# Fewer TensorE instructions in the opening of a delta-attention and two-mixture kernel, and the second solve on VectorE

## The chip, the cores and the metric

One core of a Trainium2 chip runs the kernel. The metric is the device time of one execution in microseconds, as the median of three runs. In the text PE is TensorE (PEld its weight loads), DVE VectorE, ACT ScalarE, POOL GpSimd and SP the SyncE queue that starts most transfers.

## The reference

Batch 4, 8 heads, 768 positions, head width 48. For each head a 48 x 48 state is walked through in time:

```
y[t]   = q[t] @ state
state += beta[t] * outer(k_n[t], v[t] - k_n[t] @ state)     # k_n is k over its norm
x  = y as 3072 x 384
x  = (silu(x @ w_gate) * (x @ w_val)) @ w_out               # 384 -> 1536 -> 384
out = mish(x @ w_in) @ w2_out                               # 384 -> 2048 -> 384
```

The weights come as float64 and are made float32 on the chip.

## The kernel before, in words

The sequence is cut into chunks of 32 positions; 4 batches of 32 make 128 partitions. Three chunks are a step (t = 0 to 7). Inside a chunk the recurrence is a triangular system: from the grams of k with k (`gram_pair`) a solve on VectorE gives a 32 x 32 inverse for each head and chunk. The grams of k with q become the matrix p, masked on GpSimd (`att_mask`). Then, chunk after chunk: `read` (k and q times the state, labels r and y), the v that remains, `att_solved` (z, the inverse times v), `att_out` (p times z added to y, label o), `att_update` (k times z added to the state, label u), and `x_out` (the output transposed and split into a high and a low part, xh and xl, label x).

The first mixture runs one step behind: step t's twelve gate and value groups (g0, v0, g1, ...: nine matmuls each, three products of high and low parts) and downs (x0, x1, ...) stand on TensorE while step t+1's attention is put between them. Each group's result leaves one PSUM bank: g by ScalarE (s), v by VectorE (h). The weights of the first mixture are 36 pieces, each made from float64 in passes: two on ScalarE (`conv_begin`, tile raw), one on VectorE (`conv_step`, tile f, L572), a high part on ScalarE (w1h, L591) and a low part on GpSimd (w1l, L592).

The order is written by hand. `START` is a list of words for the opening, taken one after the other: each word issues its instructions, on whichever engines, in this order, and each engine's queue keeps it. `kg0` is the k grams of chunk 0, `Kg0` those of step 1, `qg0` k with q; `sq`, `norm`, `turn`, `scale`, `diag` prepare the solve; `s2` is two steps of step 0's solve on VectorE, `P5` five steps of step 1's on GpSimd, `S` the same on VectorE; the solve is done in halves (`solve_half`, 15 steps, L276 and L283) and the quarter that joins the halves is made by TensorE (`ja`, `jb`; `Ja`, `Jb` for step 1); `back` transposes the result (L287 to L289); `vs` multiplies v by the norm on GpSimd, `qm` masks p there; `cb`, `d`, `t` are conversion passes; `h12` is twelve warm-up matmuls. `z0>` begins a word (its matmuls), `>z0` goes on with it (its evacuation). `EARLY1` names words due at a time counted in groups of the first mixture's step 0 (0.7 is near the end of g0). `plan` gives due times to the other steps. DMA starts stand on SP's queue, the first ten weight fetches on ScalarE's (`FETCH`).

The prediction's terms go through `START`, `EARLY1`, `att_mask` (L195), `square_sums` (L206), `att_solved` (L365), `att_out` (L384), `att_update` (L402), `gram_pair` (L449) and the loads after L791.

Of the kernel before, what the change touches and what calls it, by code (L numbers as in the profile page):

```python
# [7 lines left out]
F32 = mybir.dt.float32  # L8
# [5 lines left out]
ALU = mybir.AluOpType  # L14
# [10 lines left out]
FIRST = 0  # L25
FB = 3
START = """
sq0 sq1 sq2 h12 kg0 kg1 norm kg2 turn0 scale diag s1 Kg0 s2 Kg1 s2 Kg2 s2 qg0 s2 qg1 s2 qg2 s5 vs0 vs1 vs2 fetch go cb2 qm0 qm1 qm2 back0 clear
ja0> ja1> >ja0 jb0> ja2> >ja1 turn1 nb d1 >jb0 z0> >ja2 jb1> ns1 y0 >z0 u0> o0> ns2 t1 >u0 >jb1 r1> jb2> y1 ne >r1 z1> gam1 >o0 >jb2 x0> d1 >z1 u1> o1> scale diag >x0 >x0 t1 P5
>u1 r2> y2 >r2 z2> >o1 x1> d1 >z2 u2> o2> >x1 >x1 P5 t1 >u2 >o2 x2> qg3 >x2 >x2 P5 d1 t1 qm3 d1 t1 done  # L30
"""
FILL = (0.1, 0.8)
W2AT = (4.5, 2.0, 6)
W2F = 2.0
W2G = 1.7
RAWS = 2
FETCH = 10
RAWB = 4
MOST = 2
GRAMS = ("g", "x20", "x21", "x22") * 5  # L40
JOINS = ("x21", "x22") * 3
XTS = ("v", "x22", "v")
AHEAD = 1
EARLY1 = "0.7:back1 1.3:Ja0> 1.3:Ja1> 1.6:>Ja0 1.6:>Ja1 2.3:Ja2> 2.3:Jb0> 2.6:>Ja2 2.6:>Jb0 3.3:Jb1> 3.3:Jb2> 3.6:>Jb1 3.6:>Jb2 4.0:qg4 4.6:qm4 6.3:qg5 7.3:qm5"
GRAM2 = 6.0


# [12 lines left out]
def tile_delta_attention_moe_moe(  # L60
# [54 lines left out]
    w1h, w1l = [list(x) + [None] * 3 for x in zip(*map(w1_tiles, range(J1 - 3)))]  # L115
# [20 lines left out]
    ss, rs, n_sys = [t_tmp[:, C * i:C * i + C] for i in range(3)]  # L136
    state = at.tile([128, B, NP, 2, D], F32, name="state")

    z_s = at.tile([128, H, 2, D], F32, name="z_s")
    y_s = [at.tile([128, DM], F32, name=f"y{i}") for i in range(NCH)]  # L140

    w2d = [dram.tile([128, 6, 128], F32, name=f"w2d{j}") for j in range(J2)]
# [37 lines left out]
    def k_of(n):  # L180
        return lent_k if n == 2 else k_s[n % 2]
# [11 lines left out]
    spare = {"gram": list(GRAMS), "join": list(JOINS), "xt": list(XTS)}  # L193

    def att_mask(t, c):  # L195
        p = p_nat[num(t, c) % 5]
        nc.gpsimd.tensor_tensor(
            out=p, in0=p, in1=mask.unsqueeze(1).to_broadcast([128, H, C]), op=ALU.mult
        )

    def turn_g(t):
        nc.vector.transpose(
# [1 line left out]
        )  # L204

    def square_sums(c):  # L206
        sq = m1.tile([128, H, D], F32, tag="h", name="sq")
        kk = k_of(c)
        nc.vector.tensor_tensor(out=sq, in0=kk, in1=kk, op=ALU.mult)
        nc.vector.tensor_reduce(out=n_nat[:, c * H:c * H + H], in_=sq, op=ALU.add, axis=mybir.AxisListType.X)  # L210

    def norms(diag):
# [151 lines left out]
    @phased  # L364
    def att_solved(t, c):  # L365
        z = psa.tile([128, H, D], F32, tag="a", name="z")
        for h in range(H):
            for b in range(B):
                bs = slice(C * b, C * b + C)
                nc.tensor.matmul(  # L370
                    out=z[bs, h], lhsT=t_of(t)[bs, :, c * H + h], rhs=v_s[c][bs, h, :], start=True, stop=True
                )
        yield
        for x in range(2):
            if starting and x:
                nc.vector.tensor_scalar(
                    out=z_s[:, :, x, :], in0=z, scalar1=turn_of[:, x:x + 1], scalar2=None, op0=ALU.mult
                )
            else:
                nc.scalar.activation(out=z_s[:, :, x, :], in_=z, func=AF.Identity, scale=turn_of[:, x:x + 1])  # L380
        load(1, num(t + 1, c))

    @phased
    def att_out(t, c, hold):  # L384
        y = hold["y"]
        for h in range(H):
            for b in range(B):
# [61 lines left out]
    def gram_pair(t, c, which=(0, 1), raw=False):  # L449
        n = num(t, c)  # L450
        ws = slice(which[0], which[-1] + 1)
        pss = [bank([128, NP, 2, C], "gram") for _ in range(2)]
        for p in range(NP):
            for b in range(B):
                bs = slice(C * b, C * b + C)
                for par in range(2):
                    rows = slice(64 * par, 64 * par + D)
                    nc.tensor.matmul(  # L458
                        out=pss[par][bs, p, ws],
                        lhsT=kq_of(n)[rows, p, 0, bs],  # L460
                        rhs=kq_of(n)[rows, p, ws, bs],
                        start=True,
                        stop=True,
                    )
# [338 lines left out]
    for b in range(B):
        ub = upper[C * b:C * b + C, :]
# [40 lines left out]
    def solve_next(t, n, eng):  # L845
# [231 lines left out]
```

## Time and profile before

| | us |
|---|---|
| median of three runs (1077.42 to 1078.47) | 1077.65 |
| the profiled execution | 1075.51 |
| its span, first to last instruction | 1073.4 |
| TensorE busy (96% of the span) | 1031.5 |
| VectorE busy (48%) | 512.9 |
| ScalarE busy (37%) | 398.3 |
| GpSimd busy (18%) | 190.2 |

Matmul times are modelled and overlap, so a busy TensorE is not at its peak. A row of the timeline gives start, length, engine, line, operation, what is written and read, count, and in brackets the idle time of the engine before it with what ended it; "issue" means that the profile shows no wait. The granted clock is a share of 2.4 GHz; 0.50 is the lower level, 1.2 GHz.

### The profile page before, as it was taken

To read this page: it belongs to the slowest core of one execution; us is meant where nothing else is said; L and a number is where in the kernel's file an instruction comes from. 1 tells how busy PE (TensorE), PEld (TensorE's weight loads), DVE (VectorE), ACT (ScalarE), POOL (GpSimd) and SP (SyncE) were. 2 spreads that over 40 slices of the span, in tenths; PEclk is the share of its full clock that TensorE was granted. 3 is DMA by queue.
4 is the path that set the end of the run, shared out by engine and by line. 5 is a ranking of instruction groups with operands and counts; after the bars stand their busy time and mean duration, and the time that the engine had idled before them with its cause. 6 is when DMAs were issued, how large, how long until landed. Compare 5 with 4: busy or idle time off the path is not lost.

```text
span 1073.4 us, 29430 instructions
## 1 busy us (share of the span) xinstructions
PE 1031.5 (96%) x12980; PEld 988.7 (92%) x12980; DVE 512.9 (48%) x1113; ACT 398.3 (37%) x871; POOL 190.2 (18%) x222
## 2 busy tenths in 40 slices
PE   4779799999999999999999999999999999999998
PEld 4668699889989999999999999999999999999998
DVE  8555896785884885866852243212121222212111
ACT  2259744224224234243222345333333333323232
POOL 3276632211211312212211121000000000000000
PEclk6779899999999999999999999999999999999999
DMA  7246624215206125132010044001000000100000
GB/s 213 93 152 211 202 85 154 72 45 167 72 32 188 45 72 154 44 109 68 16 60 2 16 148 140 23 7 39 24 23 23 23 31 16 38 7 30 1 23 23
DMA packets 43183, 77.52 MB, mean 72 GB/s; under 512 B 4272, under 2 KB 30000, under 8 KB 43056
## 3 DMA queue, kind: packets, MB, share of 16 engines
q1 hardware_dynamic: 41904, 72.50, 21.6%
q10 hardware_dynamic: 1152, 3.15, 0.9%
q8 instruction: 102, 1.67, 0.7%
q14 instruction: 25, 0.20, 0.1%
HBM read 59.90 MB, written 15.73 MB: 70 GB/s over the span
## 4 chain that ended last, share of the span: by engine, by line
PE 81%; DVE 6%; issue 1%; ACT 1%; ACTq 0%; DVEq 0%
PE o L635 19%; PE h L635 19%; PE v L635 12%; PE x L707 12%; PE g L635 11%; PE z L370 1%; PE ks L350 1%; PE ds L412 1%; PE y L389 1%; PE y L350 1%; DVE t_tmp L324 1%; PE gram L458 1%; DVE t_sys L331 1%; DVE h L686 1%; DVE state L429 1%
## 5 line engine op out<-in xcount | busy, mean ns | idle before, releaser
L983 DVE TENSOR_TENSOR gl<-gg,gh 128x384 fp32r<-128x384 f32 x128 | 71.4, 558 | 319.2 <-ACT gh L982 319.2
L692 POOL TENSOR_TENSOR hp<-h,hp 128x384 fp32r<-128x384 f32 x96 | 99.8, 1039 | 419.4 <-ACT hp L691 419.4
L977 ACT ACTIVATE gg<-h 128x384 f32<-128x384 f32 x128 | 62.9, 492 | 264.8 <-PE h L635 264.8
L707 PE MATMUL x<-hp,w1h 128*128 128x384 f32 x576 | 132.1, 338 | 1.4 <-ACT hp L691 1.4
L635 PE MATMUL o<-w2l,gh 128*128 128x384 f32 x384 | 129.3, 337 | 0.0
L635 PE MATMUL o<-w2h,gh 128*128 128x384 f32 x384 | 129.2, 336 | 0.0
L635 PE MATMUL o<-w2h,gl 128*128 128x384 f32 x384 | 129.2, 336 | 0.0
L691 ACT CAST hp<-h 128x384 fp32r<-128x384 f32 x96 | 49.3, 513 | 168.5 <-DVE h L686 168.4
L707 PEld LDWEIGHTS x<-hp,w1h 128*128 128x128 f32 x576 | 101.1, 188 | 3.9 <-ACT hp L691 2.1
L635 PE MATMUL h<-x2h,w2h 128*128 128x384 f32 x384 | 88.0, 337 | 0.0
L635 PE MATMUL h<-x2l,w2h 128*128 128x384 f32 x384 | 87.8, 336 | 0.0
L635 PE MATMUL h<-x2h,w2l 128*128 128x384 f32 x384 | 87.7, 336 | 0.0
L686 DVE TENSOR_TENSOR h<-s,v 128x384 f32<-128x384 f32 x96 | 52.8, 549 | 72.7 <-PE v L635 72.1
L678 ACT ACTIVATE s<-g 128x384 f32<-128x384 f32 x96 | 46.9, 489 | 101.6 <-PE g L635 101.6
L324 DVE TENSOR_TENSOR t_tmp<-t_sys,g_sys 128x31 f32<-128x31 f32 (+15 forms) x186 | 80.9, 435 | 4.5
L331 DVE TENSOR_TENSOR t_sys<-t_sys,t_tmp 128x31 f32<-128x31 f32 (+15 forms) x186 | 74.8, 402 | 6.4
L635 PE MATMUL g<-xh,w1h 128*128 128x384 f32 x288 | 69.2, 349 | 7.5 <-ACT s L678 6.5
L635 PEld LDWEIGHTS o<-w2h,gh 128*128 128x128 f32 x384 | 72.1, 188 | 0.0
L635 PEld LDWEIGHTS o<-w2h,gl 128*128 128x128 f32 x384 | 72.1, 188 | 0.0
L635 PEld LDWEIGHTS o<-w2l,gh 128*128 128x128 f32 x384 | 72.1, 188 | 0.0
L635 PE MATMUL v<-xh,w1h 128*128 128x384 f32 x288 | 67.8, 343 | 2.9 <-DVE h L686 2.6
L635 PEld LDWEIGHTS h<-x2h,w2h 128*128 128x128 f32 x384 | 68.9, 188 | 0.0
(129 smaller groups left out, 1762.9 us busy)
## 6 DMA issues: line engine op xcount, KB each, us to landing
raw<-in_w_second_dram SPq DMA_DIRECT2D x32, 384.0 KB, 4.0
raw<-in_w_first_dram SPq DMA_DIRECT2D x28, 384.0 KB, 3.9
kqT<-in_kq_dram SPq DMA_DIRECT2D x18, 512.0 KB, 3.6
w2d<-f SPq DMA_DIRECT2D x32, 192.0 KB, 4.1
w2raw<-w2d SPq DMA_DIRECT2D x16, 384.0 KB, 2.9
v<-in_v_dram SPq DMA_DIRECT2D x24, 192.0 KB, 2.9
x2d<-xs SPq DMA_DIRECT2D x24, 192.0 KB, 1.9
x2raw<-x2d SPq DMA_DIRECT2D x24, 192.0 KB, 2.4
```

Source lines behind the costliest of these rows:

```text
L324: nc.vector.tensor_tensor(out=tmp, in0=t_sys[:, 0:m, j:j + 1].to_broadcast([128, m, n]), in1=g_sys[:, j:j + 1, j + 1:C].to_broadcast([128, ...
L331: nc.vector.tensor_tensor(out=sl, in0=sl, in1=tmp, op=ALU.subtract)
L350: nc.tensor.matmul(out=ps[bs, 2 * p:2 * p + 2], lhsT=kqt[:, p, w, bs], rhs=state[:, b, p], start=not w or p == 0, stop=not w, skip_group_c ...
L370: nc.tensor.matmul(out=z[bs, h], lhsT=t_of(t)[bs, :, c * H + h], rhs=v_s[c][bs, h, :], start=True, stop=True)
L635: nc.tensor.matmul(out=ps, lhsT=a, rhs=b, start=start and i == 0, stop=stop and i == len(seq) - 1)
L678: nc.scalar.activation(out=s, in_=ps, func=AF.Silu)
L686: nc.vector.tensor_tensor(out=h, in0=g_t.pop(j), in1=ps, op=ALU.mult)
L691: nc.scalar.copy(out=hh, in_=h)
L692: nc.gpsimd.tensor_tensor(out=hl, in0=h, in1=hh, op=ALU.subtract)
L707: nc.tensor.matmul(out=x2[kk], lhsT=w[j][:, 6 + kk, :], rhs=m, start=j == 0 and i == 0, stop=j == J1 - 1 and i == 2,)
L977: nc.scalar.activation(out=gg, in_=ps, func=AF.Mish)
L983: nc.vector.tensor_tensor(out=gl, in0=gg, in1=gh, op=ALU.subtract)
```

## The change: what it does

- k and q are loaded together, and the grams of k with k and k with q come out of one pass with 64 columns (`kq`), for chunks 0 to 4; chunk 5 has k in the opening (`kg5`) and q in the mixture. p of the first three chunks goes into lent weight space, unmasked.
- The first three outputs (`att_out` at t = 0) use one 128 x 128 matrix for a head, which GpSimd builds as p times a block-diagonal mask of 1024 elements a partition, and 8 matmuls of 48 columns for 32 of 32 x 32 blocks; z is kept once more whole (`z_all`) for it.
- z_s is laid out by parity first, and both its halves come from ScalarE.
- The v products and masks of the opening stand behind the first solve on GpSimd. The squares of k are made by ScalarE.
- Step 1's solve is on VectorE: seven steps in the opening, eight in g0 of the mixture; its transposes come at 0.9 and its joins at 2.9 to 4.6 groups. The last state update of step 0 is added at 1.6 groups.
- jb2 stands behind z1, more warm-up matmuls stand between the grams, the weight fetches are all on SP's queue, three conversion pieces may be under way (`MOST`), and six rather than five pieces are done in the opening.

```diff
-sq0 sq1 sq2 h12 kg0 kg1 norm kg2 turn0 scale diag s1 Kg0 s2 Kg1 s2 Kg2 s2 qg0 s2 qg1 s2 qg2 s5 vs0 vs1 vs2 fetch go cb2 qm0 qm1 qm2 back0 clear
-ja0> ja1> >ja0 jb0> ja2> >ja1 turn1 nb d1 >jb0 z0> >ja2 jb1> ns1 y0 >z0 u0> o0> ns2 t1 >u0 >jb1 r1> jb2> y1 ne >r1 z1> gam1 >o0 >jb2 x0> d1 >z1 u1> o1> scale diag >x0 >x0 t1 P5
->u1 r2> y2 >r2 z2> >o1 x1> d1 >z2 u2> o2> >x1 >x1 P5 t1 >u2 >o2 x2> qg3 >x2 >x2 P5 d1 t1 qm3 d1 t1 done
+sq0 sq1 sq2 h12 kq0 kq1 norm kq2 h8 turn0 scale diag s3 kq3 h6 s3 kq4 h6 s3 kg5 h12 s6 go cb3 back0 clear vs0 qm0 vs1 qm1 vs2 qm2 qm3 qm4
+ja0> ja1> >ja0 jb0> ja2> >ja1 turn1 nb d1 >jb0 z0> >ja2 jb1> ns1 y0 >z0 u0> o0> t1 ns1 d1 >u0 >jb1 r1> y1 ns1 ne >r1 z1> >o0 jb2> gam1 scale diag S1 >z1 t1 d1 u1> o1> S2 >u1 >jb2 r2> x0> y2 t1 >x0 >r2 >x0 d1 >o1 z2> x1> >z2 t1 S2 o2> u2> >x1 >x1 >o2 x2> h4 d1 >x2 >x2 S2 t1 d1 t1 done
-FETCH = 10
+FETCH = 0
-MOST = 2
+MOST = 3
-XTS = ("v", "x22", "v")
+XTS = ("x22",) * 3
-EARLY1 = "0.7:back1 1.3:Ja0> 1.3:Ja1> 1.6:>Ja0 1.6:>Ja1 2.3:Ja2> 2.3:Jb0> 2.6:>Ja2 2.6:>Jb0 3.3:Jb1> 3.3:Jb2> 3.6:>Jb1 3.6:>Jb2 4.0:qg4 4.6:qm4 6.3:qg5 7.3:qm5"
+EARLY1 = "0.3:S4 0.6:S4 0.9:back1 1.6:>u2 2.9:Ja0> 2.9:Ja1> 3.2:>Ja0 3.2:>Ja1 3.6:Ja2> 3.6:Jb0> 3.9:>Ja2 3.9:>Jb0 4.3:Jb1> 4.3:Jb2> 4.6:>Jb1 4.6:>Jb2 6.0:qg5 6.3:qm5"
...
-    z_s = at.tile([128, H, 2, D], F32, name="z_s")
+    z_s = at.tile([128, 2, H, D], F32, name="z_s")
...
+        n = num(t, c)
+        p = p_of(n)
+        if n < NCH:
+            nc.gpsimd.tensor_tensor(
+                out=lent_p[n][:, 0:H].rearrange("q h (b t) -> q h b t", b=B),
+                in0=p.unsqueeze(2).to_broadcast([128, H, B, C]),
+                in1=same.unsqueeze(1).to_broadcast([128, H, B, C]),
+                op=ALU.mult,
+            )
...
-        nc.vector.tensor_tensor(out=sq, in0=kk, in1=kk, op=ALU.mult)
+        nc.scalar.activation(out=sq, in_=k_of(c), func=AF.Square)
...
+        if starting and c == NCH - 1:
+            nc.scalar.copy(out=z_all, in_=z)
         for x in range(2):
-            if starting and x:
-                nc.vector.tensor_scalar(
-                    out=z_s[:, :, x, :], in0=z, scalar1=turn_of[:, x:x + 1], scalar2=None, op0=ALU.mult
-                )
-            else:
-                nc.scalar.activation(out=z_s[:, :, x, :], in_=z, func=AF.Identity, scale=turn_of[:, x:x + 1])
+            nc.scalar.activation(out=z_s[:, x], in_=z, func=AF.Identity, scale=turn_of[:, x:x + 1])
+        if starting and c < NCH - 1:
+            nc.vector.tensor_copy(out=z_all, in_=z)
...
+            if t == 0:
+                nc.tensor.matmul(
+                    out=y[:, h], lhsT=lent_p[c][:, h, :], rhs=z_all[:, h, :], start=c == 0 and h == 0,
+                    stop=h % 2 == 1, skip_group_check=True,
+                )
+                continue
...
-            pss = [psm.tile([128, NP, 2, D], F32, tag=x, name="ds") for x in ("g", "x20")]
+            tags = ("x20", "x21") if c == NCH - 1 else ("g", "x20")
+            pss = [psm.tile([128, NP, 2, D], F32, tag=x, name="ds") for x in tags]
...
-        load_kq(c, slice(0, 1))
+        load_kq(c)
     nc.sync.dma_start(out=beta_s, in_=beta)
+    for c in range(NCH):
+        load(1, c)
+    for n in range(NCH, 2 * NCH):
+        load_kq(n)
+    for n in range(RAWB):
+        fetch(n)
...
-    for n in range(NCH, 2 * NCH):
-        load_kq(n, slice(0, 1))
-    for c in range(NCH):
-        load_kq(c, slice(1, 2))
-        load(1, c)
-    fetch(0, nc.sync)
-    fetch(1, nc.sync)
-    for n in range(NCH, 2 * NCH):
-        load_kq(n, slice(1, 2))
...
-        "kg": lambda n: gram_pair(0, n, (0,)),
-        "Kg": lambda n: gram_pair(1, n, (0,)),
+        "kq": lambda n: gram_pair(n // NCH, n % NCH, (0, 1), True),
+        "kg": lambda n: gram_pair(n // NCH, n % NCH, (0,)),
```

## Rows read from the trace of the kernel before

**Rows 1.** The chain that ended last: shares of the span, and in order of time (start, us):

```profile
PE 81%; DVE 6%; issue 1%; ACT 1%; ACTq 0%; DVEq 0%
...
148.07 1.56 PE v L635 x9
```

**Rows 2.** Busy time by stretch, granted clock, DMA share, GB/s; last two VectorE alone:

```profile
26.43:40.11 13.68, 9.32 (x459) 8.38 (x452) 6.64 (x19) 4.89 (x11) 1.97 (x2) 0.50 0.25 89
40.11:60.83 20.72, 13.46 (x589) 10.96 (x585) 11.21 (x27) 6.97 (x16) 11.89 (x28) 0.91 0.39 131
60.83:74.71 13.88, 12.55 (x283) 11.55 (x284) 8.25 (x13) 9.06 (x20) 9.47 (x14) 0.57 0.57 170
74.71:81.58 6.87, 6.64 (x211) 5.86 (x211) 2.09 (x5) 3.46 (x9) 4.04 (x5) 1.00 0.29 79
...
130.50:1073.40 942.90, 935.06 (x9968) 902.90 (x9968) 429.60 (x922) 327.17 (x705) 119.45 (x115) 1.00 0.19 59
...
8.00:10.00 2.00, 1.37 (x83) 1.06 (x83) 1.69 (x10) 1.20 (x4) 0.00 (x0) 0.50 1.12 309
...
16.76:23.80 7.04, 6.36 (x20) 0.50 0.42 107
...
65.25:67.88 2.63, 2.63 (x5) 0.50 0.66 214
```

**Rows 3.** Timeline of TensorE, from the opening to the stop before g8:

```profile
13.24 1.78 PE L458 MATMUL gram<-kqT 48*32 48x32 f32 x127 [3.39 <-issue]
18.84 0.74 PE L458 MATMUL gram<-kqT 48*32 48x32 f32 x47 [3.82 <-issue]
...
26.12 1.89 PE L298 MATMUL join<-lent_tn,g_nat 32*32 32x16 f32 x113 [0.68 <-issue]
...
30.02 0.91 PE L298 MATMUL join<-lent,tT_nat 32*32 32x16 f32 x49 [1.79 <-issue]
...
44.85 0.54 PE L370 MATMUL z<-v,lent_tn 32*32 32x48 f32 x19 [0.59 <-issue]
...
57.07 0.55 PE L440 MATMUL xt<-ident,y 128*128 128x128 f32 x3 [0.60 <-ACT y L398]
...
59.41 0.46 PE L458 MATMUL gram<-kqT 48*32 48x32 f32 x29 [1.38 <-issue]
...
60.83 1.33 PE L635 MATMUL g<-xh,w1h 128*128 128x384 f32 x3 [0.96 <-ACT xh L445]
...
130.50 1.33 PE L635 MATMUL g<-xh,w1h 128*128 128x384 f32 x3 [5.38 <-ACT s L678]
```

**Rows 4.** DMA queues of the page: packets, MB, share of 16 engines:

```profile
q8 instruction: 102, 1.67, 0.7%
```

**Rows 5.** Timeline of VectorE:

```profile
13.99 0.24 DVE L276 TENSOR_TENSOR t_tmp<-t_sys,g_sys 128x78 f32<-128x78 f32 x1
14.27 0.75 DVE L283 TENSOR_TENSOR t_sys<-t_sys,t_tmp 128x78 f32<-128x78 f32 x1
...
55.71 2.07 DVE L429 TENSOR_TENSOR state<-state,ds 48x384 f32<-48x384 f32 x4 [0.52 <-PE ds L412]
...
114.04 0.94 DVE L219 TENSOR_SCALAR t_tmp<-t_tmp 128x32 uint32<-128x32 uint32 x1
115.02 0.18 DVE L222 TENSOR_SCALAR t_tmp<-t_tmp 128x32 uint32<-128x32 uint32 x1
```

**Rows 6.** Timeline of GpSimd:

```profile
14.02 0.90 POOL L314 TENSOR_TENSOR v<-v,n_nat 128x384 f32<-128x384 f32 x1 [7.28 <-DVE t_sys L283]
...
20.79 0.72 POOL L197 TENSOR_TENSOR p<-p,mask 128x256 f32<-128x256 f32 x1 [3.22 <-ACT p L471]
...
26.49 0.96 POOL L870 MEMSET t_sys<- 128x1024 f32 x1 [1.00 <-DVE lent_tn L289]
...
113.92 1.02 POOL L592 TENSOR_TENSOR w1l<-f,w1h 128x384 fp32r<-128x384 f32 x1
```

**Rows 7.** Timeline of ScalarE:

```profile
60.28 0.50 ACT L445 CAST xh<-xt 128x384 fp32r<-128x384 f32 x1
```

More of the change, by code (lines that the diff above doesn't have):

```diff
@@ L113, in w1_tiles @@
         return [pool.tile([128, 9, 128], F32R, tag=f"{x}{j}", name=f"w1{x}{j}") for x in "hl"]
-    w1h, w1l = [list(x) + [None] * 3 for x in zip(*map(w1_tiles, range(J1 - 3)))]
+    w1h, w1l = [list(x) + [None] * 5 for x in zip(*map(w1_tiles, range(J1 - 5)))]
     k_s = [at.tile([128, H, D], F32, name=f"k{i}") for i in range(2)]
@@ L172, in tile_delta_attention_moe_moe, with p_of @@
     lent_tn = lent_tn[:, 0:C * 32].rearrange("p (a b) -> p a b", a=C)
+    lent_p = [w1.tile([128, 9, 128], F32, tag=x, name=f"lent_p{x}") for x in ("l9", "h8", "l8")]
+    same = lent_p[0][:, 8, :].rearrange("p (b t) -> p b t", b=B)
+    lent_w = w1.tile([128, 9, 128], F32, tag="h7", name="lent_w")
+    z_all = lent_w[:, 0:3].rearrange("p a b -> p (a b)").rearrange("p (h d) -> p h d", h=H)
+    lent_raw = [
+        lent_w[:, 3 + 2 * i:5 + 2 * i].rearrange("p a b -> p (a b)").rearrange("p (h t) -> p h t", h=H)
+        for i in range(NCH)
+    ]
+    def p_of(n):
+        return lent_raw[n] if n < NCH else p_nat[n % 5]
     def t_of(t):
@@ L195, in att_mask @@
     def att_mask(t, c):
-        p = p_nat[num(t, c) % 5]
-        nc.gpsimd.tensor_tensor(
-            out=p, in0=p, in1=mask.unsqueeze(1).to_broadcast([128, H, C]), op=ALU.mult
-        )
+        n = num(t, c)
[7 more added lines that the diff above has]
+            )
+        else:
+            nc.gpsimd.tensor_tensor(
+                out=p, in0=p, in1=mask.unsqueeze(1).to_broadcast([128, H, C]), op=ALU.mult
+            )
     def turn_g(t):
@@ L206, in square_sums @@
     def square_sums(c):
-        sq = m1.tile([128, H, D], F32, tag="h", name="sq")
-        kk = k_of(c)
-        nc.vector.tensor_tensor(out=sq, in0=kk, in1=kk, op=ALU.mult)
+        sq = m1.tile([128, 2, N], F32, tag="hp", name="sq", bufs=2)
+        sq = sq[:, 0].rearrange("p (h d) -> p h d", h=H)
+        nc.scalar.activation(out=sq, in_=k_of(c), func=AF.Square)
         nc.vector.tensor_reduce(out=n_nat[:, c * H:c * H + H], in_=sq, op=ALU.add, axis=mybir.AxisListType.X)
@@ L373, in att_solved @@
         yield
+        if starting and c == NCH - 1:
+            nc.scalar.copy(out=z_all, in_=z)
         for x in range(2):
-            if starting and x:
-                nc.vector.tensor_scalar(
-                    out=z_s[:, :, x, :], in0=z, scalar1=turn_of[:, x:x + 1], scalar2=None, op0=ALU.mult
-                )
-            else:
-                nc.scalar.activation(out=z_s[:, :, x, :], in_=z, func=AF.Identity, scale=turn_of[:, x:x + 1])
+            nc.scalar.activation(out=z_s[:, x], in_=z, func=AF.Identity, scale=turn_of[:, x:x + 1])
+        if starting and c < NCH - 1:
+            nc.vector.tensor_copy(out=z_all, in_=z)
         load(1, num(t + 1, c))
@@ L386, in att_out @@
         for h in range(H):
+            if t == 0:
+                nc.tensor.matmul(
+                    out=y[:, h], lhsT=lent_p[c][:, h, :], rhs=z_all[:, h, :], start=c == 0 and h == 0,
+                    stop=h % 2 == 1, skip_group_check=True,
+                )
+                continue
             for b in range(B):
@@ L391, in att_out @@
                     lhsT=p_nat[num(t, c) % 5][bs, h, :],
-                    rhs=z_s[bs, h, b % 2, :],
-                    start=(t == 0 and c == 0 and h == 0),
+                    rhs=z_s[bs, b % 2, h, :],
+                    start=False,
                     stop=(h % 2 == 1),
@@ L414, in att_update @@
                         lhsT=k_of(n)[rows, 2 * p + par, :],
-                        rhs=z_s[rows, 2 * p + par],
+                        rhs=z_s[rows, :, 2 * p + par, :],
                         start=True,
@@ L465, in gram_pair @@
         gv = g_of(t)[:, :, 0:CH].rearrange("q t (c p w) -> q w c p t", c=NCH, w=2)
-        pv = p_nat[n % 5].rearrange("q (p w) t -> q w p t", w=2)
+        pv = p_of(n).rearrange("q (p w) t -> q w p t", w=2)
         for par in range(2):
@@ L469, in gram_pair @@
                 nc.scalar.copy(out=gv[:, par, c], in_=pss[par][:, :, 0, :])
+        for par in range(2):
             if 1 in which and raw:
@@ L801, in tile_delta_attention_moe_moe @@
         )
+    nc.gpsimd.memset(same, 0.0)
+    for b in range(B):
+        bs = slice(C * b, C * b + C)
+        nc.gpsimd.tensor_copy(out=same[bs, b, :], in_=mask[bs, :])
     nc.gpsimd.memset(upper, -1.0)
```

## The prediction

> **What bounds the kernel now.** I began with the chain that ended last: TensorE holds 81% of it, VectorE 6%, and pauses without a visible cause 1% [rows 1]. The table by stretch then says where TensorE isn't full [rows 2]. From 130.50 us to the end it is busy 935 of 943 us at full clock, so time gained or lost earlier passes to the end one for one. The loss lies in four stretches: from the start to 26.43 (the first solve and its transposes end), to 40.11 (the first read of the state, "r1"), to 60.83 (the first mixture matmul, "g0"), to 74.71 (the second value group, "v1"). From there to 81.58 ("g2") TensorE is again nearly full.
>
> TensorE's own rows show two kinds of wait [rows 3]. Some have a name, as the cast that g0 waits for. Others read "issue", and they come after 127 or 128 matmuls: 127 from 13.24, then 3.82 of pause. A matmul comes with a weight load, which makes 256 instructions, and the queue of kind "instruction" carried 1.67 MB in 102 packets, so blocks of 16 KB [rows 4]. I read it so: a block is asked for as the one before it is entered, and is there 3.9 us later (26.12 to 30.02), or 5.6 while the loads fill the DMA engines (13.24 to 18.84). Where TensorE runs 128 matmuls faster than that, it waits: 3.82 and 1.79 there, 0.59 at 44.85, 1.38 at 59.41.
>
> The rows of VectorE and GpSimd show a third kind [rows 5, 6]. A solve step takes 0.24 at 13.99, and the next, of the same size, 0.75 at 14.27, until GpSimd's v product (0.90 from 14.02) has ended. A norm step at 114.04 takes 0.94 where its neighbour takes 0.18 (115.02), until GpSimd's w1l (from 113.92) has ended. So a VectorE step on SBUF alone waits out a GpSimd product, one for each step.
>
> **The change, term by term** (after less before, us).
>
> *To the end of the solve: -1.2.* The squares go to ScalarE. That shortens the norm, but the last grams end later than the norm: they will wait for k and q together, three halves of 0.26 MB more ahead of the third, 2.5 us at 309 GB/s [rows 2], less what longer rows in memory save. I take 0.9 (bounds 0 and 1.7). In the solve four steps lost 2.1 to v products (0.51 of it at 14.27); those now come after it: -2.1. Grams ahead of the solve's end fall from 576 matmuls to 384, and 32 warm-ups come in; both lie beside VectorE's solve. If that cover failed, the last twelve warm-ups at half clock, 0.35 each (twice 1.56 for nine [rows 1]), would put up to 4.2 on the path. The weight fetches that leave ScalarE's queue for SP's stand behind the key loads, four at once, and land before the solve ends.
>
> *From there to r1: 13.7 now, 15.3 then, +1.7.* GpSimd now has in one row: clearing t_sys 0.96, three v products of 0.90, three masks of 1024 elements, two of 256 at 0.72, and a w1l of 1.02 [rows 6]. No row has a mask of 1024. By 0.72 for 256 and 1.02 for 384 it would be 2.5, by 0.72 and 0.90 1.8; I take 2.3, nearer the first, whose reads are alike. Sum 13.0, and 0.55 where GpSimd waits for VectorE's f in turn. Beside it VectorE has, in order, three norm steps, an f, the first join's sum, three norm steps, a copy of z, three more, an f, and the state's copy on which r1 waits. Each step on SBUF lets a GpSimd product pass first, so VectorE gets through with GpSimd's queue: 13.55, then 0.2, 0.55 and half a state, 1.04 by the four sums at 55.71 [rows 5]. Bounds -1.0 and +1.1 about this by the mask's length, and -4.7 if nothing waits (TensorE's blocks decide then: the second join would end near 29.0, z0 near 32.8).
>
> *From r1 to g0: 20.7 now, 17.6 then, -3.1.* The grams qg3 leave. Now they follow the last transposes, which end at 57.62, with a pause of 1.38 in them, and ScalarE casts x2 only at 60.28, behind their copies: -2.6 [rows 3, 7]. The join jb2 (1.07 by 1.89 for 113 matmuls at 26.12) goes behind z1, and z1's pause of 0.59 goes: -1.7. Added: two solve steps ahead of the state sums, one of them behind a w1l, +0.7; a copy of z ahead of the last y copy, 0.50 like the cast at 60.28, +0.5. The last outputs need 16 matmuls for 64; TensorE waits for ScalarE there, so nothing. Bounds -4.3 without the additions, -1.2 if the pauses fall elsewhere.
>
> *From g0 to v1: 13.9 now, 16.6 then, +2.7.* v1 needs the bank that h0 empties, and h0 stands on VectorE behind all that is due before it. New there is the solve, which ran on GpSimd beside the rest, and the state sums. After the split of x2 (0.55) come ten solve steps (7.04 now, 1.09 of it waits: 5.95), four f of 0.6, the transposes 2.63, the state sums 2.07, h0 0.55: 14.2 [rows 2, 5]. Three w1l meet solve steps, 0.8 of each 1.02: 2.4. TensorE meanwhile has three groups and two joins. Bounds +0.3 (no such meeting) and +3.3.
>
> *From v1 to g2: +1.8.* Four joins follow where two did, +2.1, with gaps +2.3, and the grams qg4 (1.0 by 64 matmuls) are gone: +1.3. TensorE has by then waited 3 us or more twice; over 60.83 to 74.71, with shorter waits, the granted clock was 0.57 [rows 2], a mixture of 1.2 and 2.4 GHz. A third of v1 at the lower level is +0.5. Bounds 0.4 and 3.5.
>
> *Afterwards: 0.* The stop of 5.38 ahead of 130.50 [rows 3] hangs on VectorE's order in the next step's set-up, which stays; one more weight piece ahead (MOST) doesn't shorten that. Bounds -2 and +2.
>
> Sum -1.2 + 1.7 - 3.1 + 2.7 + 1.8 = +1.9. The profiled execution took 1075.51 (span 1073.4 and 2.1 around it), 2.1 under the median 1077.65: 1077.4 for such a run, 1079.6 for the median.
>
> A rule speaks against the first idea of the change. The Trainium skill, "Runtime: NRT & Kernel Launch", section "Instruction fetch mechanics", says that TensorE holds 2048 instructions and that fetching the next 16 KB block is mostly hidden. The trace differs from it, with pauses after every 256 instructions; by the rows the 1.38 and the 0.59 go with the instructions, by the rule they have another cause and could stay, and the sum would be +3.9.
>
> **Rivals.**
> *A, faster:* VectorE slips between GpSimd's products, in the opening and from g0 to v1. Then TensorE's blocks set the opening, and its missing matmuls show (1653 by the words of the list, 1289 then: nearly three blocks): -4.7, and up to -2.4 more, so 1072.5 to 1074.9. For it: pauses as long as 3.82 [rows 3]. Against: the steps at 14.27 and 114.04 [rows 5]. It decides if z0 begins before 31.
> *B, slower:* the clock. TensorE, starved before the early joins and again before v1, stays at half speed through v1, x0 and g2: 1.56 more for each, 4.7 where I took 0.5, so 1083.8. It decides from a wait before v1 of 4 us. For: 0.57 in the stretch to 74.71. Against: 1.00 right after it [rows 2].
> *C:* the pauses aren't code, and stay in qg3's place and in z1: 1081.6. The steady 127 or 128 speaks against it. That page would have it so.
>
> **How the numbers follow.** A measurement of this kernel can tell about 0.2%, 2.2 us. My case has 0.42 (1077.5 to 1082; 0.26 within 2.2 us of no change, 0.16 above), A 0.33, B 0.20, C 0.05 (0.02 and 0.03). Faster 0.33, same 0.28, slower 0.39. The range takes in A's and B's prices with the bounds of the mask and of the afterwards: 1071 to 1084.
>
> **What would show it.** Right: no pause in a last gram, g0 near 58; r1 at 40 to 41, with norm steps of 1 to 2.3 us beside the masks; h0 some 15.5 after the split of x2, and TensorE idle before v1. Wrong: r1 before 38, or masks under 1.5; v1 before 71; a stop near g8 far from 5.4, for then the later stage answers and not the opening.

## The result, and the profile after

The changed kernel takes 1085.70 us (median of four runs, 1083.91 to 1086.69), the kernel before 1077.73 in the same comparison: a ratio of 1.0071, with a 95% interval of 1.0054 to 1.0089. That is 8 us more, outside the forecast range of 1071 to 1084. The profiled execution took 1085.68 (span 1083.9), so its own time is the median, where that of before stood 2.1 under its median. The stretches of the two profiles therefore add up to 10.5 more, where the medians differ by 8.0 and the forecast for the profiles was 1.9; in which stretch before's profile was lucky, no row shows.

The stages end at the same events as in the prediction; "step 1's x" is the first group of nine transposes of step 1's output, behind which the two kernels run alike.

| stretch | before | after | forecast | measured |
|---|---|---|---|---|
| start to the end of the solve's transposes | 26.43 | 25.60 | -1.2 | -0.8 |
| to r1 | 13.68 | 14.79 | +1.7 | +1.1 |
| r1 to g0 | 20.72 | 20.95 | **-3.1** | **+0.2** |
| g0 to v1 | 13.88 | 15.85 | +2.7 | +2.0 |
| v1 to g2 | 6.87 | 10.82 | **+1.8** | **+4.0** |
| g2 to step 1's x | 70.49 | 74.12 | **0** | **+3.6** |
| from there to the end | 921.33 | 921.77 | 0 | +0.4 |

The busy time by stretch of the changed kernel, as in [rows 2] (columns: length, then busy time of PE, PEld, DVE, ACT and POOL with counts, granted clock, DMA share, GB/s):

```profile
25.60:40.39 14.79, 11.11 (x385) 10.22 (x377) 14.50 (x18) 5.31 (x12) 13.07 (x10) 0.63 0.15 46
40.39:61.34 20.95, 17.64 (x429) 15.20 (x429) 13.10 (x36) 8.89 (x20) 3.02 (x3) 0.77 0.40 136
61.34:77.19 15.85, 8.70 (x156) 7.83 (x155) 15.12 (x34) 6.20 (x14) 4.02 (x4) 0.68 0.34 110
77.19:88.01 10.82, 10.52 (x274) 9.51 (x275) 4.39 (x8) 8.01 (x19) 8.41 (x9) 0.50 0.47 153
```

To r1, VectorE is busy 14.50 of 14.79 and GpSimd 13.07, where before had 6.64 and 1.97 of 13.68: the two run as one queue (busy time holds the time in which a step is held up). From g0 to v1 VectorE is busy 15.12 of 15.85 and TensorE 8.70; before it was 8.25 and 12.55. So VectorE has become the bound from the first solve to r1 and from g0 to v1; between the two it is busy 13.10 of 20.95, and what counts there is when it reaches the state sums. After v1 TensorE is busy and the clock is 0.50.

TensorE's timeline of the changed kernel, which answers to [rows 3]:

```profile
15.32 1.10 PE L485 MATMUL gram<-kqT 48*32 48x64 f32 x55 [0.67 <-issue]
20.90 0.86 PE L855 MATMUL heat<-cold 128*128 128x384 f32 x4 [0.72 <-issue]
...
28.38 0.45 PE L319 MATMUL join<-lent,tT_nat 32*32 32x16 f32 x18 [0.94 <-issue]
30.84 1.81 PE L391 MATMUL z<-v,lent_tn 32*32 32x48 f32 x63 [1.04 <-POOL lent_pl L211]
...
35.40 3.65 PE L408 MATMUL y<-lent_w,lent_pl 128*128 128x48 f32 x16
40.39 1.51 PE L371 MATMUL ks<-state,kqT 128*32 128x96 f32 x32 [1.34 <-DVE state L454]
...
50.69 1.88 PE L371 MATMUL ks<-state,kqT 128*32 128x96 f32 x32 [2.42 <-DVE state L456]
...
69.22 1.33 PE L663 MATMUL g<-xh,w1h 128*128 128x384 f32 x3 [4.48 <-ACT s L706]
...
77.19 1.33 PE L663 MATMUL v<-xh,w1h 128*128 128x384 f32 x3 [2.68 <-DVE h L714]
...
139.44 1.33 PE L663 MATMUL g<-xh,w1h 128*128 128x384 f32 x3 [4.25 <-ACT s L706]
```

The page's row of the instruction queue, against [rows 4]:

```profile
q8 instruction: 98, 1.61, 0.6%
```

Four blocks fewer are fetched. In this profile the pauses that read "issue" have shrunk from 3.82, 1.79 and 1.38 to under 1, and none is left behind 28.38. Their size is not steady: e1, an experiment below with the same opening, has one of 2.24 among the warm-ups, beside VectorE's solve, and 0.44 and 0.64 in z0.

```profile
20.66 0.98 PE L855 MATMUL heat<-cold 128*128 128x384 f32 x4 [2.24 <-issue]
```

From r1 to g0 none of the seven profiles with these outputs has such a pause, so there the change did what it says. In place of the pauses stand waits for VectorE (1.34, 2.42, 2.68) and, ahead of g1, 4.48 for ScalarE, whose evacuation of g0 at 68.70 stood behind a conversion that waited for VectorE's f and then for raw data.

VectorE's timeline of the changed kernel (against [rows 5]):

```profile
27.71 2.28 DVE L243 TENSOR_SCALAR t_tmp<-t_tmp 128x32 uint32<-128x32 uint32 x1
...
31.23 2.28 DVE L250 SCALAR_TENSOR_TENSOR t_tmp<-t_tmp 128x32 f32<-128x32 f32 x1
...
39.22 1.11 DVE L454 COPY state<-ds 48x384 f32<-48x384 f32 x2
...
40.89 0.19 DVE L250 SCALAR_TENSOR_TENSOR t_tmp<-t_tmp 128x32 f32<-128x32 f32 x1
...
45.45 0.56 DVE L400 COPY lent_w<-z 128x384 f32<-128x384 f32 x1 [0.87 <-ACT z_s L398]
45.92 1.39 DVE L600 SCALAR_TENSOR_TENSOR f<-raw 128x384 uint32<-128x384 uint32 x1
...
48.00 1.04 DVE L304 TENSOR_TENSOR t_sys<-t_sys,t_tmp 128x78 f32<-128x78 f32 x1
48.97 2.05 DVE L456 TENSOR_TENSOR state<-state,ds 48x384 f32<-48x384 f32 x4
```

GpSimd's timeline beside it (against [rows 6]):

```profile
27.61 2.35 POOL L211 TENSOR_TENSOR lent_pl<-lent_w,lent_pl 128x1024 f32<-128x1024 f32 x1
...
31.11 2.35 POOL L211 TENSOR_TENSOR lent_ph<-lent_w,lent_pl 128x1024 f32<-128x1024 f32 x1
...
45.89 1.01 POOL L620 TENSOR_TENSOR w1l<-f,w1h 128x384 fp32r<-128x384 f32 x1 [7.02 <-ACT w1h L619]
47.94 1.01 POOL L620 TENSOR_TENSOR w1l<-f,w1h 128x384 fp32r<-128x384 f32 x1 [1.04 <-ACT w1h L619]
```

A norm step that takes 0.19 when nothing is beside it (L250 at 40.89) takes 2.28 beside a mask (at 31.23) and ends with it: 31.23 + 2.28 and 31.11 + 2.35. The mask of 1024 elements takes 2.35; the prediction took 2.3. At 45.45 a copy of z, new on VectorE, waits 0.87 for ScalarE's z_s; the conversion f and two pairs of solve steps stand behind it, and now meet two w1l (45.89 and 47.94). So the state sums begin at 48.97, and r2 waits for them.

The Trainium skill, "SBUF — State Buffer", section "Who interferes with whom", says that a VectorE instruction with two inputs in SBUF, or in a mode that uses both port pairs, and a GpSimd instruction that reads SBUF share one lock, and that the later of the two is blocked fully. The trace agrees for a step with two inputs: L250 takes 0.19 alone and 2.28 beside a product of 2.35. The step at 27.71 has one input and is held up as well (27.71 + 2.28 and 27.61 + 2.35); no row tells its mode.

### The profile page after: what moved, and what is told of

The parts are those of the page before. It is cut to its first block, busy times and chain, and to the rows that moved or that the text cites. A ratio compares the mean times of both kernels' runs of the same rounds, so it can differ in the third digit from the quotient of the medians.

```text
span 1083.9 us, 28572 instructions
## 1 busy us (share of the span) xinstructions
PE 1048.0 (97%) x12552; PEld 1002.7 (93%) x12552; DVE 527.5 (49%) x1139; ACT 401.0 (37%) x878; POOL 184.2 (17%) x197
## 4 chain that ended last, share of the span: by engine, by line
PE 83%; DVE 10%; ACT 2%; DMA 2%; issue 2%; SPq 0%; DVEq 0%; ACTq 0%
PE o L663 19%; PE h L663 19%; PE v L663 12%; PE x L735 12%; PE g L663 12%; PE z L391 2%; PE ks L371 2%; PE y L371 2%; PE ds L439 1%; PE y L415 1%; PE gram L485 1%; DMA raw<-in_w_first_dram 1%; DVE t_tmp L345 1%; DVE t_sys L352 1%; DVE h L714 1%
```

## The experiments

Four theories are told apart: the depth of the conversion (`MOST`, D), step 1's solve on VectorE (V), the first outputs with their masks and copies of z, and the clock (K). Each time is a median beside runs of the kernel before on the same chip; stretches come from the matmul rows of the one profiled execution. None of the kernels leaves anything out; the three on the clock add idle matmuls.

| kernel | us | ratio to before (95%) | r1 to g0 | g0 to v1 | v1 to g2 | g2 to step 1's x |
|---|---|---|---|---|---|---|
| before | | 1 | 20.72 | 13.88 | 6.87 | 70.49 |
| changed | 1085.70 | 1.0071 (1.0054 to 1.0089) | 20.95 | 15.85 | 10.82 | 74.12 |
| e1 | 1082.80 | 1.0059 (1.0043 to 1.0075) | 20.86 | 15.86 | 10.83 | 70.77 |
| e2 | 1086.53 | 1.0095 (1.0073 to 1.0116) | 20.66 | 15.88 | 10.83 | 73.18 |
| e3 | 1078.51 | 1.0022 (1.0012 to 1.0031) | | | | |
| e4 | 1081.72 | 1.0041 (1.0027 to 1.0055) | 17.36 | 15.88 | 10.82 | 74.65 |
| e5 | 1084.36 | 1.0067 (1.0052 to 1.0082) | 19.42 | 15.89 | 10.82 | 74.27 |
| e6 | 1083.39 | 1.0061 (1.0042 to 1.0079) | 20.75 | 15.99 | 10.03 | 74.51 |
| e7 | 1070.76 | 0.9945 (0.9925 to 0.9964) | 18.53 | 14.85 | 5.74 | 71.00 |
| e8 | 1078.62 | 1.0009 (0.9996 to 1.0022) | 18.50 | 15.86 | 10.83 | 72.29 |
| e9 | 1075.36 | 0.9979 (0.9964 to 0.9994) | 20.86 | 11.02 | 7.47 | 73.22 |
| e10 | 1085.93 | 1.0078 (1.0065 to 1.0090) | 21.29 | 15.89 | 10.83 | 74.27 |
| e11 | 1072.11 | 0.9951 (0.9936 to 0.9966) | 19.30 | 11.94 | 7.95 | 71.53 |
| e12 | 1082.10 | 1.0041 (1.0026 to 1.0056) | 17.39 | 15.89 | 10.81 | 73.47 |
| e13 | 1082.58 | 1.0050 (1.0032 to 1.0068) | 16.45 | 15.89 | 10.82 | 72.82 |
| e14 | 1074.68 | 0.9977 (0.9968 to 0.9987) | 21.15 | 12.25 | 6.75 | 70.60 |
| e15 | 1071.76 | 0.9952 (0.9939 to 0.9965) | 18.31 | 15.22 | 5.73 | 70.97 |

The two stretches after g0 hardly move from kernel to kernel unless the part that sets them is changed: wherever the solve is on VectorE they are 15.9 to 16.0 and 10.8 (10.03 in e6, with its idle matmuls). The profiled execution of e3 was the longest of its ten, 1083.07 where the median is 1078.51, so its stretches are left out.

**First batch: one part undone at a time.**

e1, the changed kernel with two pieces under way:

```diff
-MOST = 3
+MOST = 2
```

> The changed kernel with MOST = 2 again. Theory D (depth): with three weight pieces in conversion only one of the four raw buffers is left for a transfer, so each fetch of about 4.5 us stands on the path; the 3.6 us lost between g2 and the end of step 0 come from it: 1085.7 falls by 2 to 4, and g2 to the first transposes takes 70.5 again in place of 74.1. Rival: the loss there comes only from TensorE's clock and VectorE's order, and 1085.7 stays within 1.

The last stretch is back to 70.77 from 74.12; the time is 2.9 less by the medians and 1.3 by the ratios, whose intervals overlap. So the trace bears out the depth, the times alone don't settle it (e8 does, below).

e2, 24 idle matmuls between v0 and g1, to keep the clock up:

```diff
-... 1.6:>u2 2.9:Ja0> ...
+... 1.6:>u2 1.95:H24 2.9:Ja0> ...
```

> The changed kernel with 24 idle-time matmuls of 384 columns between v0 and g1, where TensorE waits 4.5 us; nothing else moves. Theory K (clock): the granted clock stays at 1.0 until v1, v1 to g2 falls from 10.8 to about 8, and the time by 2 to 4 although work is added. Rival: the stretch is bound by VectorE's queue alone, and the time stays or rises by up to 1.

The clock stayed at 1.00 from 56 to 76 us, then fell in the wait before v1 (3.07), and v1 to g2 stayed at 10.83. The time rose by 2.6 by the ratios, within the intervals. The idle matmuls cover only one of the two waits, so this is a miss, not a verdict on the clock.

e3, step 1's solve back on GpSimd, the early words at the times of before:

```diff
-gam1 scale diag S1 >z1 ... o1> S2 >u1 ... t1 S2 o2> u2> ... >x2 S2 t1 d1
+gam1 scale diag >z1 ... o1> P5 >u1 ... t1 P5 o2> u2> ... >x2 P5 t1 >u2 d1
```

> The changed kernel with step 1's solve on GpSimd and the early words of the mixture at their times of before. Theory V (VectorE's backlog): v1 comes at most 14 after g0 (15.9 now), no wait of 4.5 ahead of g1; the time falls by 4 to 7, to 1079 to 1082. Rival (the clock falls anyway, the opening is what costs): it falls by less than 2.

5.3 us less by the ratios (0.49% of 1077), with intervals that don't touch. The place of the solve, with the words that go with it (transposes, joins and last state sum), is the largest single part. The expected stretch was not seen: in the one profile v1 comes 17.19 after g0, where at most 14 was expected, and as that execution was 4.6 over the median it settles neither.

e4, the first outputs as before: 32 x 32 blocks, masks of 256 elements, no copy of z:

```diff
-    out=lent_p[n][:, 0:H].rearrange("q h (b t) -> q h b t", b=B),
-    in0=p.unsqueeze(2).to_broadcast([128, H, B, C]),
-    in1=same.unsqueeze(1).to_broadcast([128, H, B, C]),
+    out=p, in0=p, in1=mask.unsqueeze(1).to_broadcast([128, H, C])
...
-lhsT=lent_p[c][:, h, :], rhs=z_all[:, h, :]
+lhsT=p_of(num(t, c))[bs, h, :], rhs=z_s[bs, b % 2, h, :]
-nc.scalar.copy(out=z_all, in_=z)
-nc.vector.tensor_copy(out=z_all, in_=z)
```

> The changed kernel with the first outputs from 32 x 32 blocks and masks of 256 elements again (no copy of z). Theory M (masks block the norm): GpSimd's row between the solve and r1 loses three times 1.6, so r1 comes at 35 to 37 in place of 40.4, g0 3 to 5 earlier, and the time falls by 3 to 5. Rival (TensorE's instruction blocks decide once there are 144 matmuls more): r1 at 38 or later, time within 1.5.

r1 comes at 38.83 for 40.39, later than expected, as a pause without a visible cause of 1.85 now stands in z0; with the masks short, TensorE's blocks are the next limit:

```profile
34.04 0.61 PE L384 MATMUL z<-v,lent_tn 32*32 32x48 f32 x17 [1.85 <-issue]
```

And r1 to g0 is 17.36, which is what the prediction had (17.6); e8, with the same opening, has 18.50. So what failed there lies in the new form of the outputs; which part of it, e10 to e13 had to tell.

**Second batch: the clock, and the parts together.**

e5, twelve idle matmuls behind o1:

```diff
-u1> o1> S2 >u1
+u1> o1> h12 S2 >u1
```

> The changed kernel with twelve warm-up matmuls behind o1, where TensorE waits 2.4 us for the state. Theory K (clock): the granted clock stays at 1.0 over r2, y2 and z2, which took 1.88, 1.51 and 1.51 at half of it; r2 to g0 (10.65 now) falls to 8 to 8.5, and the time by 1.5 to 2.5. Rival: the stretch is set by VectorE and ScalarE, r2 to g0 stays above 10, time within 1.

The clock held 1.00 from 46 to 68 us, where the changed kernel had 0.50 from 50 to 56. The busy time by stretch, first of the changed kernel, then of e5:

```profile
50.00:52.00 2.00, 1.31 (x28) 1.15 (x30) 1.40 (x3) 0.00 (x0) 0.00 (x0) 0.50 0.18 65
50.00:52.00 2.00, 1.73 (x23) 1.22 (x25) 1.95 (x5) 0.00 (x0) 0.00 (x0) 1.00 0.51 195
```

From r2 to g0 it took 8.84 for 10.65: the lower clock cost 1.8 there. The end moved by 0.4 by the ratios, inside the intervals.

e6, 24 idle matmuls before g1 and 18 before v1:

```diff
-... 1.6:>u2 2.9:Ja0> 2.9:Ja1> 3.2:>Ja0 ...
+... 1.6:>u2 1.95:H24 2.9:Ja0> 2.9:Ja1> 2.95:W18 3.2:>Ja0 ...
```

> The changed kernel with idle-time matmuls at both waits of the early mixture, 24 ahead of g1 and 18 between the joins and v1 (the run with the first alone left the clock at 1.0 until 75 us; it fell in the second wait). Theory K: v1, x0 and g2 run at full clock, v1 to g2 takes 8 in place of 10.8, and the time falls by 2 to 4. Rival: after v1 the evacuations on VectorE and ScalarE set the pace, time within 1.

Two stretches of the busy time by stretch, first of the changed kernel:

```profile
76.00:78.00 2.00, 0.81 (x2) 0.81 (x3) 1.97 (x4) 0.83 (x2) 0.24 (x1) 0.50 0.62 198
78.00:80.00 2.00, 1.70 (x21) 1.20 (x21) 0.07 (x1) 2.00 (x7) 2.00 (x3) 0.50 0.89 269
```

then of e6:

```profile
76.00:78.00 2.00, 2.00 (x13) 1.93 (x12) 1.94 (x5) 0.60 (x2) 0.00 (x1) 1.00 0.76 240
78.00:80.00 2.00, 0.74 (x6) 0.42 (x4) 0.31 (x1) 2.00 (x6) 2.00 (x3) 1.00 0.84 212
82.00:84.00 2.00, 2.00 (x46) 1.57 (x43) 1.42 (x3) 0.56 (x3) 1.48 (x2) 0.71 0.08 25
```

At full clock v1 is done sooner, and then TensorE waits (0.74 busy from 78 to 80, with ScalarE and GpSimd busy 2.00 of 2.00), 1.26 of it for ScalarE's evacuation of a join. The clock falls again at 82 to 84. v1 to g2 is 0.8 shorter, and the last stretch 0.4 longer; the time is 1.1 less by the ratios, inside the intervals. So with the solve on VectorE holding the clock gave back only a small part; a kernel that does so and holds it all the way to g2 wasn't made.

e7, small outputs, depth two, and the solve on GpSimd, each undone at once:

```diff
-MOST = 3
+MOST = 2
-gam1 scale diag S1 >z1 ... u1> o1> S2 >u1 ... t1 S2 o2> u2> ... S2 t1 d1
+gam1 scale diag >z1 ... u1> o1> P15 >u1 ... t1 o2> u2> ... t1 >u2 d1
```

(with the diff of e4, and step 1's transposes and joins at the times of before).

> The changed kernel with three parts undone: masks of 256 and 32 x 32 blocks for the first outputs, MOST = 2, and step 1's solve on GpSimd (fifteen steps in one row behind u1, joins at their times of before). Theory: the three losses stand at different places and add up (-4, -3, -6): 1072 to 1075, under the kernel before. Rival: they share VectorE's queue and only the largest shows: 1077 to 1080.

1070.76, 0.55% under the kernel before. TensorE's timeline of e7 shows what is left:

```profile
62.38 2.12 PE L312 MATMUL join<-t_nat,lent_g 32*32 32x16 f32 x128 [3.17 <-DVE t_nat L301]
...
126.17 1.33 PE L646 MATMUL g<-xh,w1h 128*128 128x384 f32 x3 [5.42 <-ACT s L689]
```

The early joins wait 3.17 for the solve's transposes (1.32 in before), and the stop ahead of g8 is the 5.4 of [rows 3].

e8, as e7 with the solve left on VectorE:

```diff
-MOST = 3
+MOST = 2
```

(with the diff of e4).

> The changed kernel with masks of 256, 32 x 32 blocks and MOST = 2, the solve left on VectorE. Theory: -4 and -3 add up, 1078 to 1080; against the run with the solve on GpSimd it shows the price of the solve on VectorE, 5 to 6. Rival (the depth only mattered behind the late masks): 1081 to 1083.

Against e4 it differs by the depth alone: 1.0009 for 1.0041, intervals that don't touch, so depth three costs 3.4 us there. Against e7 it differs by the place of the solve and the words that go with it: 1.0009 for 0.9945, 6.9 us. Of the profile's stretches, v1 to g2 holds most of it, 10.83 for 5.74.

**Third batch: depth from the other side, and the outputs taken apart.**

e9, the kernel before with three pieces under way:

```diff
-MOST = 2
+MOST = 3
```

> The kernel before with three conversion pieces under way in place of two, and nothing else. If the depth costs by itself (three pieces hold three of the four raw buffers, so each fetch is issued only when one is emptied): about 1079 to 1080, some 3 over before, as the undoing of it on the changed kernel gave 3. If the depth only costs beside the changed kernel's fetch order: within 0.7 of before.

A miss: not slower, but 0.2% quicker. The stretches show two opposite effects: from g0 to v1 it gains 2.9 (11.02), and from v1 on it loses 0.6 and 2.7. They don't explain the 0.2%, for this one profile is 1.2 longer as a whole than that of before. So depth has two effects, and in the changed kernel only the bad one shows, as its g0 to v1 is 15.85 with depth three and 15.86 with two (e1).

The chain of the changed kernel, with the length of each piece, points to what the bad one is:

```profile
104.80 4.46 DMA raw<-in_w_first_dram
110.89 4.58 DMA raw<-in_w_first_dram
129.19 4.17 DMA raw<-in_w_first_dram
```

With depth three a whole weight fetch is on the path three times (the page of the profile has 3.9 us from issue to landing): there are four raw buffers, a piece keeps its own until VectorE has read it, and so three pieces under way can leave only one for a transfer. The chains of e4 and e9 hold three such pieces each; in the chains of the seven kernels with two under way at this point there is none. In the nine profiles with depth three throughout the last stretch is 72.8 to 74.7; in the seven with two there it is 70.5 to 72.3. A fifth buffer would test it directly; it wasn't tried, so the cause is argued from the chains.

e10, large masks and copies of z kept, only the matmuls small again, one for each head and batch:

```diff
-lhsT=lent_p[c][:, h, :], rhs=z_all[:, h, :]
+lhsT=lent_p[c][bs, h, bs], rhs=z_all[bs, h, :]
```

> The changed kernel with its large masks of 1024 elements kept, and only the product p times z of the first three chunks made of 32 by 32 blocks again (64 matmuls for 16, read out of the diagonal blocks). If the long first outputs come from the 128 by 128 form of the matmul: from r1 to g0 some 18.5 to 19.5 in place of 20.95, with o1 and o2 of 0.9 at full clock, r1 at about 38.5 as o0 takes 1.5 in place of 3.65; the end 1 to 2.5 under the changed kernel, 1083.5 to 1085. If it is the masks that set the opening, through VectorE's and GpSimd's queues: r1 stays at 40.4 and the end within 0.7 of the changed kernel.

Nothing. TensorE's timeline of e10:

```profile
36.45 1.57 PE L410 MATMUL y<-lent_w,lent_pl 32*32 32x48 f32 x64
40.13 1.51 PE L371 MATMUL ks<-state,kqT 128*32 128x96 f32 x32 [2.10 <-DVE state L456]
```

The first outputs take 1.57 in place of 3.65, and r1 then waits 2.10 for the state in place of 1.34; it comes at 40.13 for 40.39, and r1 to g0 isn't shorter. The form of the matmul isn't what sets the time.

e11, as e7 with the joins one group later:

```diff
-1.3:Ja0> 1.3:Ja1> ... 3.6:>Jb1 3.6:>Jb2
+2.3:Ja0> 2.3:Ja1> ... 4.6:>Jb1 4.6:>Jb2
```

> The version that was fastest so far (first outputs in small blocks, depth two, step 1's solve on GpSimd) with step 1's joins due one group later, 2.3 to 4.6 in place of 1.3 to 3.6, so that TensorE does not stand before the joins until the solve's transposes are done (3.17 at 62.38 there). If that wait sets the early mixture: v1 2 to 3 earlier and 1068 to 1069.5 at the end. If the wait only moves to the next bank: 1070 to 1072.

g0 to v1 is 2.9 shorter, v1 to g2 2.2 longer and the time that of e7 within its interval: the wait moves. So joins a group later cost nothing that can be told, which leaves the solve itself, or the last state sum that moves with it, as what e8 pays against e7.

**Fourth batch: the copies of z.**

e12, large masks kept, small matmuls that read z_s, no copy of z:

```diff
-rhs=z_all[:, h, :]
+rhs=z_s[bs, b % 2, h, :]
-nc.scalar.copy(out=z_all, in_=z)
-nc.vector.tensor_copy(out=z_all, in_=z)
```

> As the run with large masks and small output blocks, but the blocks read z_s, and the whole copy of z (on VectorE for chunks 0 and 1, on ScalarE for chunk 2) is left out. If the copies of z set the pace after r1, by pushing a conversion pass and two solve steps behind them into a GpSimd product, so that the state sums start at 49: r1 still at about 40 (the masks set it), the state sums near 47.5, from r1 to g0 17.5 to 18.5 in place of 20.95, and 1082.5 to 1083.7 at the end. If it is the large masks that do so, by making the conversions late: from r1 to g0 20.5 or more and 1085 to 1086.

r1 stays near, at 40.97, and r1 to g0 falls to 17.39, with 1082.10. Against e10 only the copies are gone: the copies, not the masks.

e13, the 128 x 128 form and the masks kept, the copies on ScalarE:

```diff
-nc.vector.tensor_copy(out=z_all, in_=z)
+nc.scalar.copy(out=z_all, in_=z)
```

> The changed kernel with its 128 by 128 outputs and large masks kept, the two copies of z on VectorE moved to ScalarE, behind z_s. If the copies on VectorE's queue set the pace: state sums near 48, from r1 to g0 18.5 to 19.7 (the outputs of 1.99 and 3.65 stay), and 1083.5 to 1084.6 at the end. If the 128 by 128 form sets it: o1 waits for ScalarE's copy in place, r1 to g0 20.5 to 21.3, and 1085 to 1086.3.

r1 to g0 is 16.45, 4.5 less from one kind of instruction on another engine. VectorE's timeline of e13:

```profile
45.74 0.55 DVE L600 SCALAR_TENSOR_TENSOR f<-raw 128x384 uint32<-128x384 uint32 x1
...
47.65 2.06 DVE L456 TENSOR_TENSOR state<-state,ds 48x384 f32<-48x384 f32 x4 [0.43 <-PE ds L439]
```

The f takes 0.55 for 1.39, and the sums wait for TensorE, no longer TensorE for them. r2 comes 7.81 after r1 in place of 10.30, and as TensorE didn't stop, the clock stays at 1.00 behind it, so r2 to g0 takes 8.64 for 10.65. Not all of the 4.5 is gained: r1 itself comes at 41.63 for 40.39, behind pauses that read "issue" of 0.82 and 1.20 in the joins and z0, so g0 comes 3.3 sooner (58.08 for 61.34). By the ratios the time is 2.3 less than the changed kernel's, and that of e12 3.2 less; the intervals overlap, those of e12 barely.

**Fifth batch: depth where it helps.**

e14, the kernel before with three pieces until twelve are done, then two; e15 the same on e7:

```diff
-(MOST if ended[0] < n1 - 3 else 2)
+(MOST if ended[0] < 12 else 2)
```

> The kernel before with three pieces under way until twelve pieces are done (about v1), two after. If depth buys before v1 and costs after it, as before with depth three throughout showed (g0 to v1 11.0 for 13.9, from v1 to the first transposes of step 1 80.7 for 77.4): g0 to v1 near 11, then near 77.4, and 2 to 3 under before at the end, 1074.5 to 1076. If the two are one exchange (pieces made early only take the place of later ones): the sum from g0 to the transposes stays at 91.2 to 91.7 and the end within 1.2 of before.

> The version that was fastest so far (first outputs in small blocks, step 1's solve on GpSimd, joins at the times of before), with three pieces under way until twelve are done and two after, in place of two throughout. If depth buys before v1 where VectorE has no solve there: from g0 to v1 12 to 13 in place of 14.85, and 1067 to 1069.5 at the end. If it is an exchange: 1070 to 1072.

e14 keeps 1.6 of the early gain and pays nothing later (6.75 and 70.60): 2.5 us under before, interval 1.4 to 3.4. So in the stretches the two effects of depth are separate. The times don't show what the late one costs the kernel before: e9, which pays it, has 0.9979, and e14 0.9977. It is e8 against e4 that shows a price in the time. e15 gains nothing (15.22 from g0 to v1): its joins wait 3.56 for the solve on GpSimd, which more converted weights don't shorten. e7 stays the fastest, with e11 and e15 inside its interval.

## Why the prediction was wrong

**To the end of the solve: right.** The solve starts 1.15 later (forecast 0.9) and takes 8.85 for 10.95, 2.1 less as forecast. In the fourteen profiles with this opening its transposes end between 25.34 and 26.66, in three with that of before between 26.43 and 27.26.

**From there to r1: right.** The masks took 2.35, and VectorE passed through GpSimd's queue as forecast: r1 at 40.39. Rival A, which needed VectorE to slip between, is refuted by the same rows. The sign that was set for it, z0 before 31, came up all the same (30.84). It was a poor sign: the wait stands behind z0, where VectorE reaches its half of the state's copy at 39.22, 3.7 after ScalarE's half (35.56). With small masks (e4) r1 comes 1.6 sooner, and the code pauses return, as the lower bound had it, though not at the 36 that this bound gave: one pause alone took 1.85.

**From r1 to g0, "-3.1": the step that failed.** Its second half held: from z2 to g0 it is 6.57 for 8.59, -2.0, where the prediction's x2 and y terms gave -2.1. Its first half, from r1 to z2, was to be 1.0 shorter (-1.7 for jb2 and z1's pause, +0.7 for two solve steps) and is 14.38 for 12.13, 2.3 longer, so that g0 stands at 61.34 and not near 58. The prediction listed chunk 0's copy of z before r1 and chunk 2's on ScalarE, and left out chunk 1's on VectorE. That copy costs 0.56 itself; it waits 0.87 for ScalarE's pass over the same z, and moves f and the solve steps into two w1l. e13 shows the price by moving it (and chunk 0's): r1 to z2 falls to 10.19. Of the 4.5, 2.5 come up to r2, and 2.0 after it, where the clock was 0.50 because TensorE had stood still before r2; e5, which fills that stop, has 1.8 for that part alone. With it moved the stretch is 4.3 shorter than before. That equals the prediction's lower bound by luck: the bound had the additions out, and e13 keeps them and starts the stretch later.

**From g0 to v1: right.** From the start of x2's split (61.32) to the end of h0 (77.13) it is 15.81, where the terms added up to 16.6, with three solve steps held up by a w1l as forecast (1.14, 1.07 and 1.00).

**From v1 to g2: the right mechanisms, mis-sized.** Forecast +1.3 for joins less grams, and +0.5 for the clock. By the rows of both kernels the joins less grams, with a gap of 0.3, are +0.9, and the six rows of three matmuls of v1 and x0 take 6.6 for 3.5, +3.0: all at the lower clock. That is rival B's mechanism at about rival B's price for two groups (1.56 each); only the longer wait was the one before g1 (4.48), with 2.68 before v1, where B asked for 4. But e6, which keeps the clock through v1, gets back only 0.8 of it, as ScalarE and GpSimd are full there. What the rest would give at full clock throughout stays open. With the solve on GpSimd (e7) the clock is back at 1.00 from 74 us, those six rows take 3.8, and the stretch is 5.74.

**Afterwards, "0": failed.** The prediction looked only at the stop before g8 and took one more piece under way as free. The stop did shrink to 4.25, against its word that depth doesn't shorten it (with depth two it is 5.42 again, e1). But the piece isn't free: the stretch from g2 grew by 3.6, of which e1 gives back 3.3, and e8 against e4 has 3.4 in the time. That it takes a raw buffer from the transfers is what the chains point to.

**Rival C** falls: the pause in the last grams went with them, and z1's too (from r1 to g0 none of the seven profiles with these outputs has one). The Trainium skill, "Runtime: NRT & Kernel Launch", section "Instruction fetch mechanics", has the crossing of a block mostly hidden; here too the trace differs, as e4 with shorter masks shows 1.85 and e7 2.24 of it.

Against the forecast of 1.9 for the profile, 3.3 of the 8.6 missing lie from r1 to g0, 2.2 from v1 to g2 and 3.6 behind it; the other stretches add -0.5.

By the ratios the undone parts come to 3.2 (the first outputs, e4 or e12), 5.3 to 6.9 (the solve, e3 and e8 to e7) and 1.3 to 3.4 (depth, e1 and e4 to e8): 10 to 13.5 together, against 13.6 between the changed kernel (+0.71%) and e7 (-0.55%). The upper sum must come to this, as e4, e8 and e7 undo the three one after the other; undone singly they give 10. What e7 keeps of the change (grams in one pass, squares and both halves of z_s on ScalarE, v products behind the solve, jb2 behind z1, fetches on SP's queue, more warm-ups, one more early piece) is thus worth 5.9 against before; which of these brings it was not tried.

## What to carry to other kernels

List what a change adds to each engine's queue chunk by chunk, not once for a loop: one small copy in front of a state update, on the engine that makes the update, held up the next read of the state by 2.5 us and cost 2 more through the clock (at the end 2.3 by the ratios, with intervals that overlap). Moving serial work from an engine that ran beside the rest to one that the next evacuation needs cost 5 to 7 us here. A deeper pipeline over the same buffers can take them from the transfers: ask how many are left for what is in flight, stage by stage.

## What was not expected of the hardware

One matmul instruction of 128 x 128 float32 with 48 columns takes 0.12 us (the 16 of an output in 1.99 at full clock, 3.65 at half; the 8 matmuls of the code stand twice in the trace), where the 64 of 32 x 32 with the same columns take 0.88 at full clock: a quarter of the instructions, and over twice the time. The change's idea of fewer TensorE instructions thus saved no TensorE time in the outputs, though it cost none on the path either (e10).

The depth of the conversion gained 2.9 us in one stretch and lost 3.3 in the next two of the same profile (e9); a total that moves by 0.2% shows neither.
